# A hinted branch, doubles loaded behind the experts' weights, and conversions kept in their written place, in a fused attention and FFN kernel

## The chip, the cores and the metric

One core of one Trainium2 chip runs the whole program in one launch. The metric is the device time of an execution in microseconds (us). The engines are named as in the profile: PE (TensorE, matmul; PEld its weight loads, PEq or PEldq its sequencer's own rows), DVE (VectorE), ACT (ScalarE), POOL (GpSimd) and SP (the engine that issues the DMAs here).

## The reference

Four batches of 576 tokens go through an attention with random features (8 heads of 64), a layer with 8 experts of which each token takes one, and a gated FFN:

```
q_p, k_p = phi(q), phi(k)                       # exp of a projection on 128 features
attn = (q_p @ (k_p.T @ v)) / (q_p @ sum(k_p) + 1e-6)
x = attn as 2304 x 512
idx = argmax(x_normed @ emb_normed.T / tau);  gate = softmax value at idx
for e in range(8): y[idx == e] = gate * (relu(x @ w1[e]) @ w2[e])     # 512 -> 1024 -> 512
out = (silu(y @ w_gate) * (y @ w_val)) @ w_out                        # 512 -> 1536 -> 512
```

## The kernel before, in words

**Stages.** Attention and routing fill the first 165 us or so. For each batch the routing finds on the chip the expert that takes most tokens (`dom_i`) and how many tokens go to other experts (`tot_i`, their total). Then the dominant expert of each batch runs over all 576 tokens of it, one after the other (`expert`, four times). Tokens of other experts are done by `extras`: an `If` on `totals[0] > 0` with loops over batches and experts in its body. For the data here the total is zero, so the body never runs. It stands in the program between expert 0 and expert 1. Then comes phase 3 (L1069), gate and value product of the FFN in a form with seven products, in NF = 12 slices f of the hidden width, and phase 4 (L1114), the output product with 648 matmuls of 128x512.

**Precision.** A product of floats is three matmuls on pairs of reduced-precision operands. `hi_lo` makes a pair: ACT casts (L92), DVE subtracts (L93). The weights of an expert come as floats, one raw DMA of 512 KB per unit (`Expert.fetch`, L375) and one pair of L92 and L93. An expert has four units for its first layer (`mm1`, L856, each 2 x 24 matmuls) and four groups of 48 matmuls for its second (`mm2`, L875), each followed by `gated` (DVE product L887 or L890, POOL addition L888). The weights of phases 3 and 4 arrive as 64-bit floats ("doubles"): `convert` (L746) loads two of them, 512 KB each, and `words` turns them to floats with one ACT operation (L759) and six of DVE (L760 to L778). `split_y` makes the operands of phase 3 from an expert's output `y` (names `xp`, `h_all` and `over_y` on L92, L93, and L916 for the differences).

**What sets the order.** Instructions are written by a program and then placed by a scheduler, which may move one ahead of others on its engine if its inputs allow. `keep_in_program_order` takes one from this freedom. Within an engine the placed order is fixed. Hooks (`todo`) call `extras`, `ahead`, `split...`, `weights_ahead` and `seven` between the units of an expert, keyed by batch and unit. An `If` is a compare and branch on each engine (L940); with `preferred_fallthrough_block=False` the block of the false case, which holds semaphore steps and a far jump to the join, follows directly behind the compare, and the body comes after it.

**Names.** `two` and `third` are pairs of PSUM banks that `mm1` and `mm2` use in turn; `a`, `b`, `c` are the banks of phase 3; `raw` a weight's DMA buffer, `raw64` that of two doubles, `cv_t` the conversion's scratch, `wp` a pair of expert weights, `wh`, `wl`, `over_y` pairs of weights of phase 3; `h` an input tile of phase 4 read back from DRAM (`hds`). `seven(f)` makes the sums and pairs of the weights of slice f.

Of the kernel before, what the change touches and what calls it, by code (L numbers as in the profile page):

```python
# [10 lines left out]
F32 = mybir.dt.float32  # L11
# [17 lines left out]
def attention_moe_ffn_kernel(  # L29
# [59 lines left out]

    def hi_lo(hi, lo, src, lo_eng=nc.vector):  # L90

        nc.scalar.copy(hi, src)  # L92
        lo_eng.tensor_tensor(out=lo, in0=src, in1=hi.bitcast(F32), op=ALU.subtract)  # L93
# [254 lines left out]
    why = "counts and indices worked out on the chip lie in this range"  # L348
    late = {}
    n_pair = [0]  # L350
# [7 lines left out]
    class Expert:  # L358
# [13 lines left out]
        def fetch(self, low=nc.vector):  # L372
            raw = wpool.tile([128, NC * FU], F32, tag="raw", name="raw")
            src = w12[bass.ds(self.e, 1), self.n]
            nc.sync.dma_start(out=raw, in_=src.rearrange("o p f -> p (o f)"))  # L375
            if self.extra:
                w = late["cpool"].tile([128, 2, NC * FU], F32R, tag="wp", name="wp")
            else:
                w = pair_tile()
            hi_lo(w[:, 0], w[:, 1], raw, low)  # L380
            self.ready.append(w)
            self.n += 1
# [359 lines left out]
    def convert(key, *doubles, at=None):  # L742

        raw = late["w"].tile([128, 2, DM, 2], I32, tag="raw64", name="raw64")
        for j, (f, m) in enumerate(doubles):
            nc.sync.dma_start(  # L746
                out=raw[:, j], in_=w64[f, m].bitcast(I32).rearrange("p (n w) -> p n w", w=2)
            )
        if at is None:
            at = late["w"].tile([128, 2, DM], F32, tag="w32", name="w32", bufs=2)  # L750
        w32[key] = at
        n = late["n"]
        for j in range(0, 2, n):
            words(at[:, j:j + n], raw[:, j:j + n], n)

    def words(w, raw, n):
        low, high = raw[:, :, :, 0].bitcast(U32), raw[:, :, :, 1]
        t = late["t"].tile([128, n, DM], I32, tag="raw", name="cv_t")
        nc.scalar.activation(out=t.bitcast(F32), in_=high.bitcast(F32), func=AF.Abs)  # L759
        nc.vector.tensor_scalar(  # L760
            out=t.bitcast(F32), in0=t.bitcast(F32), scalar1=F64_ZERO, scalar2=None, op0=ALU.max
        )
        nc.vector.tensor_scalar(
# [53 lines left out]
    with ExitStack() as p2:  # L817
# [51 lines left out]
        def mm2(x, hs):  # L869
            w = x.weights(128)  # L870
            ps = (banks if x.extra else pair)()[:, :, 0:HB]
            for f, h in enumerate(hs):
                for n, (a, b) in enumerate(HALVES):
                    for j in range(2):
                        nc.tensor.matmul(  # L875
                            ps[:, j], w[:, a, f, :], h[:, b, j * HB:(j + 1) * HB],
                            start=(f == 0 and n == 0), stop=(f == len(hs) - 1 and n == 2),
                        )
            return ps

        def gated(x, ps, d, add):
# [7 lines left out]
            else:  # L889
                nc.vector.tensor_tensor(out=yv, in0=ps, in1=gv, op=ALU.mult)  # L890

# [14 lines left out]
        def split_y(bt):  # L906
# [5 lines left out]
            def put(q, src):  # L912
                hi_lo(factor(bt, q, 0), factor(bt, q, 1), src)

# [19 lines left out]
        def extras():  # L934
            xs[1].fetch()
            routed.close()
            late["w"] = early.enter_context(
                tc.tile_pool(name="early", bufs=1, side="right", reuse_waits="tile")
            )
            with tc.If(totals[0] > 0, preferred_fallthrough_block=False):  # L940
                for bt in range(B):
# [19 lines left out]
        def ahead(bt):  # L961
            xs[bt - 1].fetch()
            xs[bt] = Expert(bt)
            xs[bt].fetch()

        def split(bt, runs):
            parts_at[bt] += runs
# [12 lines left out]
        def split2():  # L980
# [3 lines left out]
        todo = {  # L984
            (0, 0): routing_end, (0, NU - 1): no_y, (0, NU + NC - 1): extras,
            (1, NU - 1): split0,
# [3 lines left out]
        for bt in range(B):  # L990
            hooks = {u: go for (b, u), go in todo.items() if b == bt}
            if bt < LAST:
                hooks[NU + NC - 2] = lambda: ahead(bt + 1)
# [220 lines left out]
```

## Time and profile before

| what | value |
|---|---|
| time, median of 3 runs | 799.65 us (799.28 to 800.25) |
| the profiled execution | 802.45 us, of which 800.7 us are the span of the trace |
| mean granted clock of PE | 0.985 |
| PE busy | 767.9 us, 96% of the span |
| DVE, ACT, POOL busy | 64%, 46%, 18% of the span |
| DMA | 94.12 MB, 118 GB/s on average |

PE is the engine that is busy nearly always; the others have room on average. So the rows to read are those of the places where PE stood, and of what stood on the other engines there.

### The profile page before, as it was taken

Reading aid. Unit: us, or ns where it says so; the run is one execution under the profiler, and the core shown is the slowest. Engines: PE = TensorE matmul, PEld = TensorE weight load, DVE = VectorE, ACT = ScalarE, POOL = GpSimd, SP = SyncE. Lnnn points to the kernel's source line nnn. Section 1 sums busy time; section 2 is a strip of 40 time slices with the busy share of each in tenths; the row PEclk is TensorE's granted clock in tenths of the full one; section 3 lists DMA queues with packets and bytes.
Section 4 is the critical chain, followed back from the end, with each engine's and each line's share of the span. In section 5 each row is a group of like instructions: output and inputs, shape, how many; then the busy total and the mean of one; then the engine's idle time right before and its main releaser. Section 6 shows DMA issues by size and latency. Waiting matters only on the chain. (4 is left out here: it accounts for less than half of the span.)

```text
span 800.7 us, 16008 instructions
## 1 busy us (share of the span) xinstructions
PE 767.9 (96%) x6364; PEld 718.4 (90%) x6365; DVE 515.9 (64%) x937; ACT 368.2 (46%) x856; POOL 144.3 (18%) x197
## 2 busy tenths in 40 slices
PE   9999889999599999997999999999999999999998
PEld 8778778899499999997999999999999978888886
DVE  5788999573478655586877776877877693222220
ACT  5798578571244341343555444544454632232231
POOL 3865354200001102002021111221221110000000
PEclk9999999999799999998999999999999999999999
DMA  8644642232524322401143122423433253363323
GB/s 255 225 145 153 203 160 81 65 94 72 149 69 160 106 82 94 102 27 54 32 158 117 70 80 106 165 90 105 160 117 110 86 191 108 103 202 92 101 93 117
DMA packets 35643, 94.12 MB, mean 118 GB/s; under 512 B 4432, under 2 KB 8544, under 8 KB 35560
## 3 DMA queue, kind: packets, MB, share of 16 engines
q1 hardware_dynamic: 35400, 92.99, 35.9%
q8 instruction: 52, 0.85, 0.4%
q14 instruction: 31, 0.25, 0.1%
q10 hardware_dynamic: 160, 0.02, 0.0%
HBM read 74.05 MB, written 18.95 MB: 116 GB/s over the span
## 5 line engine op out<-in xcount | busy, mean ns | idle before, releaser
L1114 PE MATMUL o_ps<-xp 128*128 128x512 f32 x648 | 147.1, 389 | 0.0
L1114 PEld LDWEIGHTS o_ps<-xp 128*128 128x128 f32 x648 | 121.6, 188 | 25.2
L93 DVE TENSOR_TENSOR xp<-h,xp 128x1024 fp32r<-128x1024 f32 (+1 forms) x36 | 34.2, 957 | 99.1 <-ACT xp L92 98.6
L492 ACT ACTIVATE ph<-two,bias 128x128 f32<-128x128 f32 x288 | 78.2, 389 | 31.1 <-DVE bias L483 20.0
L856 PE MATMUL two<-xp,wp 128*128 128x288 f32 x576 | 81.7, 301 | 9.8 <-issue 5.8
L1041 POOL TENSOR_TENSOR cc<-c,cc 128x288 f32<-128x288 f32 x48 | 48.9, 1031 | 227.5 <-issue 201.8
L856 PEld LDWEIGHTS two<-xp,wp 128*128 128x128 f32 x576 | 79.5, 193 | 10.2 <-issue 6.0
L92 ACT CAST xp<-h 128x1024 fp32r<-128x1024 f32 (+1 forms) x36 | 30.0, 838 | 95.4 <-PE o_ps L1114 78.2
L1037 ACT ACTIVATE cc<-cc 128x288 f32<-128x288 f32 x96 | 42.1, 446 | 62.3 <-DVE cc L1034 54.3
L92 ACT CAST wp<-raw 128x1024 fp32r<-128x1024 f32 x32 | 33.6, 1049 | 54.9 <-PE two L875 29.8
L1069 PE MATMUL a<-xp,over_y 128*128 128x288 f32 x360 | 57.3, 295 | 0.0
L888 POOL TENSOR_TENSOR y_f<-y_f,t 128x576 f32<-128x576 f32 x13 | 19.1, 1473 | 200.8 <-DVE t L887 200.8
L1069 PE MATMUL a<-xp,wh 128*128 128x288 f32 x240 | 50.4, 300 | 4.5 <-DVE t L887 4.5
L93 DVE TENSOR_TENSOR wp<-raw,wp 128x1024 fp32r<-128x1024 f32 x30 | 47.0, 1567 | 10.2 <-ACT wp L92 9.8
L875 PE MATMUL third<-h_all,wp 128*128 128x288 f32 x384 | 52.8, 296 | 0.0
L875 PE MATMUL two<-h_all,wp 128*128 128x288 f32 x384 | 52.0, 295 | 0.0
L875 PEld LDWEIGHTS third<-h_all,wp 128*128 128x128 f32 x384 | 51.7, 189 | 0.0
L875 PEld LDWEIGHTS two<-h_all,wp 128*128 128x128 f32 x384 | 51.4, 189 | 0.0
L1069 PEld LDWEIGHTS a<-xp,over_y 128*128 128x128 f32 x360 | 50.8, 188 | 0.3 <-ACT s L1056 0.2
L475 DVE TENSOR_REDUCE mx<-two 128x8 f32<-128x1024 f32 x36 | 43.9, 1219 | 9.8 <-PE two L465 9.4
L1069 PEld LDWEIGHTS a<-xp,wh 128*128 128x128 f32 x240 | 39.4, 193 | 4.7 <-DVE t L887 4.7
L1034 DVE TENSOR_TENSOR cc<-c,s 128x288 f32<-128x288 f32 x48 | 21.8, 453 | 30.3 <-DMA hds<-cc 26.5
(222 smaller groups left out, 1558.0 us busy)
## 6 DMA issues: line engine op xcount, KB each, us to landing
raw<-in_w_dram SPq DMA_DIRECT2D x68, 512.0 KB, 3.8
hds<-cc SPq DMA_DIRECT2D x48, 288.0 KB, 3.1
h<-hds SPq DMA_DIRECT2D x24, 512.0 KB, 3.5
q<-in_qx_dram SPq DMA_DIRECT2D x18, 512.0 KB, 3.9
k<-in_kx_dram SPq DMA_DIRECT2D x14, 512.0 KB, 3.8
v<-in_vx_dram SPq DMA_DIRECT2D x18, 276.0 KB, 3.9
out_dram<-o SPq DMA_DIRECT2D x18, 256.0 KB, 3.3
h<-hds SPq DMA_DIRECT2D x12, 128.0 KB, 2.1
```

The lines of the kernel that those rows point to most:

```text
L92: nc.scalar.copy(hi, src)
L93: lo_eng.tensor_tensor(out=lo, in0=src, in1=hi.bitcast(F32), op=ALU.subtract)
L475: nc.vector.tensor_reduce(out=mx.rearrange("p (c a) -> p a c", a=2), in_=p.rearrange("p a (h m) -> p a h m", m=M), axis=AX.X, op=ALU.max,)
L492: nc.scalar.activation(out=ph[:, h, :], in_=p[:, h % 2, h // 2 * M:(h // 2 + 1) * M], func=AF.Exp, bias=bias[:, h:h + 1],)
L856: nc.tensor.matmul(ps[:, j], w[:, a, c, f * 128:(f + 1) * 128], xv[:, c, b, j * HB:(j + 1) * HB], start=(c == 0 and n == 0), stop=(c == NC ...
L875: nc.tensor.matmul(ps[:, j], w[:, a, f, :], h[:, b, j * HB:(j + 1) * HB], start=(f == 0 and n == 0), stop=(f == len(hs) - 1 and n == 2),)
L888: nc.gpsimd.tensor_tensor(out=yv, in0=yv, in1=t, op=ALU.add)
L1034: nc.vector.tensor_tensor(out=out, in0=ps, in1=other, op=ALU.add)
L1037: nc.scalar.activation(out=x, in_=x, func=AF.Silu)
L1041: nc.gpsimd.tensor_tensor(out=cc[:, 1], in0=c22, in1=cc[:, 1], op=ALU.mult)
L1069: nc.tensor.matmul(bank_of[k], wf[f][a][:, (wq * 2 + c) * 128:(wq * 2 + c + 1) * 128], factor(bt, xq, x)[:, c], start=(k not in begun), st ...
L1114: nc.tensor.matmul(p, h[:, x, i * 128:(i + 1) * 128], wos[f][:, a], start=(f == 0 and k == 0), stop=(f == NF - 1 and k == 2),)
```

## The change

The block of the false case of the `If` now follows its default place, behind the body and next to the join, and the branch has a label. A new hook, `near_extras`, runs one group of `mm2` ahead of `extras`; it does the weight fetches that came there and in `extras`, and puts a branch hint for the label on SP, PE and DVE, each directly behind an instruction that `late["mark"]` remembers for that engine. In `convert` the loads of doubles keep their written place while the experts run (`late["n"] == 1`). In `words` the ACT operation and the first DVE operation keep their written place. In `split_y` the first of the casts keeps its own.

```diff
--- before.py
+++ after.py
@@ -87,9 +87,11 @@
         n_banks[0] += 1
         return third() if n_banks[0] % 3 == 0 else banks()
 
-    def hi_lo(hi, lo, src, lo_eng=nc.vector):
-
-        nc.scalar.copy(hi, src)
+    def hi_lo(hi, lo, src, lo_eng=nc.vector, pinned=False):
+
+        go = nc.scalar.copy(hi, src)
+        if pinned:
+            tc.keep_in_program_order(go)
         lo_eng.tensor_tensor(out=lo, in0=src, in1=hi.bitcast(F32), op=ALU.subtract)
 
 
@@ -346,7 +348,7 @@
 
     ENG = mybir.EngineType
     why = "counts and indices worked out on the chip lie in this range"
-    late = {}
+    late = {"mark": {}}
     n_pair = [0]
 
     def pair_tile():
@@ -372,7 +374,9 @@
         def fetch(self, low=nc.vector):
             raw = wpool.tile([128, NC * FU], F32, tag="raw", name="raw")
             src = w12[bass.ds(self.e, 1), self.n]
-            nc.sync.dma_start(out=raw, in_=src.rearrange("o p f -> p (o f)"))
+            late["mark"][ENG.SP] = nc.sync.dma_start(
+                out=raw, in_=src.rearrange("o p f -> p (o f)")
+            )
             if self.extra:
                 w = late["cpool"].tile([128, 2, NC * FU], F32R, tag="wp", name="wp")
             else:
@@ -743,9 +747,11 @@
 
         raw = late["w"].tile([128, 2, DM, 2], I32, tag="raw64", name="raw64")
         for j, (f, m) in enumerate(doubles):
-            nc.sync.dma_start(
+            go = nc.sync.dma_start(
                 out=raw[:, j], in_=w64[f, m].bitcast(I32).rearrange("p (n w) -> p n w", w=2)
             )
+            if late["n"] == 1:
+                tc.keep_in_program_order(go)
         if at is None:
             at = late["w"].tile([128, 2, DM], F32, tag="w32", name="w32", bufs=2)
         w32[key] = at
@@ -756,10 +762,12 @@
     def words(w, raw, n):
         low, high = raw[:, :, :, 0].bitcast(U32), raw[:, :, :, 1]
         t = late["t"].tile([128, n, DM], I32, tag="raw", name="cv_t")
-        nc.scalar.activation(out=t.bitcast(F32), in_=high.bitcast(F32), func=AF.Abs)
-        nc.vector.tensor_scalar(
+        tc.keep_in_program_order(
+            nc.scalar.activation(out=t.bitcast(F32), in_=high.bitcast(F32), func=AF.Abs)
+        )
+        tc.keep_in_program_order(nc.vector.tensor_scalar(
             out=t.bitcast(F32), in0=t.bitcast(F32), scalar1=F64_ZERO, scalar2=None, op0=ALU.max
-        )
+        ))
         nc.vector.tensor_scalar(
             out=t, in0=t, scalar1=0x07FFFFFF, scalar2=3,
             op0=ALU.bitwise_and, op1=ALU.logical_shift_left,
@@ -872,7 +880,7 @@
             for f, h in enumerate(hs):
                 for n, (a, b) in enumerate(HALVES):
                     for j in range(2):
-                        nc.tensor.matmul(
+                        late["mark"][ENG.PE] = nc.tensor.matmul(
                             ps[:, j], w[:, a, f, :], h[:, b, j * HB:(j + 1) * HB],
                             start=(f == 0 and n == 0), stop=(f == len(hs) - 1 and n == 2),
                         )
@@ -887,7 +895,9 @@
                 nc.vector.tensor_tensor(out=t, in0=ps, in1=gv, op=ALU.mult)
                 nc.gpsimd.tensor_tensor(out=yv, in0=yv, in1=t, op=ALU.add)
             else:
-                nc.vector.tensor_tensor(out=yv, in0=ps, in1=gv, op=ALU.mult)
+                late["mark"][ENG.DVE] = nc.vector.tensor_tensor(
+                    out=yv, in0=ps, in1=gv, op=ALU.mult
+                )
 
         def expert(x, add, hooks=()):
 
@@ -910,7 +920,7 @@
             b21, b22 = y[:, 2:4, 0:HB], y[:, 2:4, HB:S]
 
             def put(q, src):
-                hi_lo(factor(bt, q, 0), factor(bt, q, 1), src)
+                hi_lo(factor(bt, q, 0), factor(bt, q, 1), src, pinned=q == 0)
 
             def sub(out, x, y):
                 nc.vector.tensor_tensor(out=out, in0=x, in1=y, op=ALU.subtract)
@@ -932,12 +942,11 @@
         totals, ends = [], []
 
         def extras():
-            xs[1].fetch()
             routed.close()
             late["w"] = early.enter_context(
                 tc.tile_pool(name="early", bufs=1, side="right", reuse_waits="tile")
             )
-            with tc.If(totals[0] > 0, preferred_fallthrough_block=False):
+            with tc.If(totals[0] > 0, label="extras"):
                 for bt in range(B):
                     with tc.For_i(0, E) as e:
                         n = nc.values_load(
@@ -963,6 +972,13 @@
             xs[bt] = Expert(bt)
             xs[bt].fetch()
 
+        def near_extras():
+            ahead(1)
+            xs[1].fetch()
+            for eng, ins in late["mark"].items():
+                with tc.issue_after(ins.ins):
+                    tc.mark_branch_hint_location("extras", "LikelyTaken", engines=[eng])
+
         def split(bt, runs):
             parts_at[bt] += runs
             ends.append(split_y(bt))
@@ -982,14 +998,15 @@
             split(2, own + [over_h(0), over_h(1)])
 
         todo = {
-            (0, 0): routing_end, (0, NU - 1): no_y, (0, NU + NC - 1): extras,
+            (0, 0): routing_end, (0, NU - 1): no_y,
+            (0, NU + NC - 2): near_extras, (0, NU + NC - 1): extras,
             (1, NU - 1): split0,
             (2, 0): lambda: weights_ahead(0), (2, NU - 1): split1,
             (3, 0): lambda: weights_ahead(1), (3, NU - 1): split2, (3, NU + 1): lambda: seven(0),
         }
         for bt in range(B):
             hooks = {u: go for (b, u), go in todo.items() if b == bt}
-            if bt < LAST:
+            if 0 < bt < LAST:
                 hooks[NU + NC - 2] = lambda: ahead(bt + 1)
             expert(xs[bt], bt > 0, hooks)
         next(ends[2], None)
```

PE around the branch, before: the end of expert 0, the load of the total, the two branches of the `If` (L940), and, past the body, expert 1.

```order
L875 MATMUL two<-h_all,wp 128x288 x96
L875 MATMUL third<-h_all,wp 128x288 x48
L953 TENSOR_LOAD tot_i
L940 COMPARE_AND_BRANCH
L940 UNCONDITIONAL_BRANCH
...
L942 REGISTER_ALU
L942 COMPARE_AND_BRANCH
L942 UNCONDITIONAL_BRANCH
L856 MATMUL two<-xp,wp 128x288 x48
```

After (the `If` is L949, `mm2` L883, `mm1` L864):

```order
L883 MATMUL two<-h_all,wp 128x288 x96
L1227 BRANCH_PREFETCH_HINT
L883 MATMUL third<-h_all,wp 128x288 x48
L962 TENSOR_LOAD tot_i
L949 COMPARE_AND_BRANCH
...
L951 COMPARE_AND_BRANCH
L951 UNCONDITIONAL_BRANCH
L949 UNCONDITIONAL_BRANCH
L864 MATMUL two<-xp,wp 128x288 x48
```

The hint stands between the last two groups of `mm2`; the unconditional branch has gone from behind the compare, and one stands behind the body.

DVE at the end of expert 3, before: conversion steps (L760 to L778), the split of y (L93, L916) and the last two products (L887).

```order
L774 SCALAR_TENSOR_TENSOR cv_t<-raw_7015 128x1024
L778 TENSOR_TENSOR w_7018<-w_7018,cv_t 128x1024
L93 TENSOR_TENSOR h_all<-y_f,h_all 128x576 x2
L916 TENSOR_TENSOR y_f<-y_f 128x2x288
L760 TENSOR_SCALAR cv_t<-cv_t 128x1024
L93 TENSOR_TENSOR h_all<-y_f,h_all 128x576
L763 TENSOR_SCALAR cv_t<-cv_t 128x1024
L887 TENSOR_TENSOR t<-two,gate 128x576
L887 TENSOR_TENSOR t<-third,gate 128x576
```

After (split L95 and L926, products L895):

```order
L95 TENSOR_TENSOR wp<-raw,wp 128x1024
L95 TENSOR_TENSOR h_all<-y_f,h_all 128x576 x2
L926 TENSOR_TENSOR y_f<-y_f 128x2x288
L95 TENSOR_TENSOR h_all<-y_f,h_all 128x576
L895 TENSOR_TENSOR t<-two,gate 128x576
L895 TENSOR_TENSOR t<-third,gate 128x576
L926 TENSOR_TENSOR y_f<-y_f 128x2x288
```

The conversion steps are gone from ahead of and between the splits; the last two products stand next to each other as before, with one split ahead of them.

DVE at the start of phase 4, before: the last two evictions of phase 3 (L1040), one conversion, the splits of two w pairs and of the input tiles h, which go on alone from there.

```order
L1040 TENSOR_TENSOR cc<-a,cc 128x288
L760 TENSOR_SCALAR cv_t<-cv_t 128x1024
...
L778 TENSOR_TENSOR w_10201<-w_10201,cv_t 128x1024
L93 TENSOR_TENSOR xp<-w_10201,xp 128x512 x2
L93 TENSOR_TENSOR xp<-h_10094,xp 128x1024
L93 TENSOR_TENSOR xp<-h_10138,xp 128x1024
L93 TENSOR_TENSOR xp<-h_10166,xp 128x1024
```

After (L1057; conversions L768 to L786):

```order
L1057 TENSOR_TENSOR cc<-a,cc 128x288 x2
L768 TENSOR_SCALAR cv_t<-cv_t 128x1024
L771 TENSOR_SCALAR cv_t<-cv_t 128x1024
...
L786 TENSOR_TENSOR w_9984<-w_9984,cv_t 128x1024
L95 TENSOR_TENSOR xp<-h_10097,xp 128x1024
L95 TENSOR_TENSOR xp<-w_9984,xp 128x512 x2
L768 TENSOR_SCALAR cv_t<-cv_t 128x1024
...
L95 TENSOR_TENSOR xp<-h_10141,xp 128x1024
L775 SCALAR_TENSOR_TENSOR w_10132<-raw_10129,cv_t 128x1024
...
L95 TENSOR_TENSOR xp<-h_10169,xp 128x1024
L95 TENSOR_TENSOR xp<-w_10132,xp 128x512 x2
L768 TENSOR_SCALAR cv_t<-cv_t 128x1024
...
L95 TENSOR_TENSOR xp<-h_10213,xp 128x1024
L775 SCALAR_TENSOR_TENSOR w_10204<-raw_10201,cv_t 128x1024
...
L95 TENSOR_TENSOR xp<-h_10241,xp 128x1024
```

Three conversions now stand among the splits of h, where one stood ahead of them. On SP the loads of the first doubles moved likewise, from behind the gates of expert 1 to behind the first weight load of expert 2.

## Rows read from the trace of the kernel before

**Rows 1.** Page, busy us of each engine (share of the span), number of instructions.

```profile
PE 767.9 (96%) x6364; PEld 718.4 (90%) x6365; DVE 515.9 (64%) x937; ACT 368.2 (46%) x856; POOL 144.3 (18%) x197
```

**Rows 2.** What PE waited for: sum of us, times, longest.

```profile
PE two L856 <- issue: 5.8, 1, 5.8
PE a L1069 <- DVE t L887: 4.5, 1, 4.5
PE two L856 <- ACT xp L92: 3.9, 1, 3.9
...
PE a L1069 <- DVE c L1034: 1.5, 2, 1.0
PE a L1069 <- ACT u L1058: 1.4, 1, 1.4
```

**Rows 3.** Timeline of PE, 190 to 232: start, us, count, [idle before, releaser].

```profile
189.72 10.29 PE L875 MATMUL two<-h_all,wp 128*128 128x288 f32 x76
199.86 6.56 PE L875 MATMUL third<-h_all,wp 128*128 128x288 f32 x48
210.33 1.57 PE L856 MATMUL two<-xp,wp 128*128 128x288 f32 x7 [3.92 <-ACT xp L92]
217.76 7.08 PE L856 MATMUL two<-xp,wp 128*128 128x288 f32 x41 [5.85 <-issue]
224.68 3.36 PE L856 MATMUL third<-xp,wp 128*128 128x288 f32 x24
```

**Rows 4.** By windows: busy us and counts of engines, PEclk, DMA share, GB/s.

```profile
212.00:224.00 12.00, 6.24 (x36) 6.24 (x36) 4.29 (x6) 1.03 (x2) 0.00 (x0) 0.62 0.45 143
...
371.00:385.00 14.00, 9.55 (x55) 9.32 (x54) 8.44 (x13) 5.35 (x11) 2.80 (x2) 0.76 0.00 0
385.00:540.00 155.00, 155.00 (x1172) 154.79 (x1172) 119.15 (x219) 75.98 (x177) 27.43 (x28) 1.00 0.30 105
```

**Rows 5.** Instructions of L940, the `If`: ns min/median/max, first to last start.

```profile
L940 DVEq COMPARE_BRANCH  x2: 51/53/55, 201.8 to 202.6; - x2
...
L940 PEldq COMPARE_BRANCH  x2: 95/1752/3410, 204.5 to 206.8; - x2
L940 PEldq EVENT_SEMAPHORE  x2: 51/51/51, 206.5 to 206.6; - x2
```

**Rows 6.** DMA issues by SP, 196 to 232.

```profile
202.55 1.07 SPq L375 DMA_DIRECT2D raw<-in_w_dram  x2
...
209.24 0.98 SPq L746 DMA_DIRECT2D raw<-in_w_dram  x2
```

**Rows 7.** Timeline of PE, 360 to 386.

```profile
370.63 1.20 PE L875 MATMUL third<-h_all,wp 128*128 128x288 f32 x8
376.29 0.85 PE L1069 MATMUL a<-xp,wh 128*128 128x288 f32 x2 [4.45 <-DVE t L887]
...
381.49 0.45 PE L1069 MATMUL c<-over_y,wh 128*128 128x288 f32 x2
```

**Rows 8.** Timeline of DVE, 366 to 384.

```profile
371.24 0.70 DVE L760 TENSOR_SCALAR cv_t<-cv_t 128x1024 f32<-128x1024 f32 x1 [2.78 <-ACT cv_t L759]
...
373.12 0.75 DVE L887 TENSOR_TENSOR t<-two,gate 128x576 f32<-128x576 f32 x1
375.47 0.76 DVE L887 TENSOR_TENSOR t<-third,gate 128x576 f32<-128x576 f32 x1 [1.60 <-POOL y_f L888]
```

**Rows 9.** Timeline of POOL, 370 to 384.

```profile
374.05 1.40 POOL L888 TENSOR_TENSOR y_f<-y_f,t 128x576 f32<-128x576 f32 x1 [11.28 <-DVE t L887]
```

**Rows 10.** Timeline of PE, 553 to 558.

```profile
556.15 1.07 PE L1069 MATMUL a<-h_all,over_y 128*128 128x288 f32 x6 [1.39 <-ACT u L1058]
```

**Rows 11.** Timeline of DVE, 640 to 700: first and last step of one conversion.

```profile
652.81 0.70 DVE L760 TENSOR_SCALAR cv_t<-cv_t 128x1024 f32<-128x1024 f32 x1 [0.21 <-ACT cv_t L759]
...
658.00 1.23 DVE L778 TENSOR_TENSOR w<-w,cv_t 128x1024 f32<-128x1024 f32 x1
```

**Rows 12.** Timeline of DVE, 640 to 700: a split of an h tile.

```profile
667.33 1.22 DVE L93 TENSOR_TENSOR xp<-h,xp 128x1024 fp32r<-128x1024 f32 x1 [3.59 <-ACT xp L92]
```

## The prediction

> **What bounds the kernel now.** I read the page's table of busy time first: TensorE (PE) is busy 767.9 of 800.7 us [rows 1], so 32.8 us are the most that filling its gaps can return (a slower clock behind a gap comes on top). Second came the list of what PE waited for: the three largest entries, 5.8 us on "issue", 4.5 us on DVE's product `t`, 3.9 us on "ACT xp" [rows 2], are single events, and they are the ones this change touches. The other entries lie in the attention stage, which the change leaves alone, or are short ones at the end of a phase. Third, the PE timeline around the two places where these three stand, and fourth the other engines there.
>
> *Place one, the branch behind expert 0.* The last group of expert 0 starts at 199.86; at 0.133 us a matmul (10.14 us for the 76 before it) its 48 end at 206.26, and the first 48 of expert 1 could be through at 212.66. The group behind those starts at 224.68 [rows 3]. The loss is 12.0 us: two idle stretches, 3.92 and 5.85, and 2.25 us of slow running (granted clock 0.62 in 212 to 224 [rows 4], where 1.00 is the upper of the two levels, 2.4 GHz, and the lower, 1.2 GHz, is 0.50). The rows of the `If` tell what the first stretch is. The compare at 204.5 must be the one of 0.095 us, since the semaphore steps start 2 us later; so the other branch, from 206.8, took 3.41 us, to 210.2, and PE's first matmul is at 210.33. DVE's two, at 201.8 to 202.6, show 0.05 us [rows 5]. The timeline blames "ACT xp", but the program's first matmul there needs nothing of ACT that late; I read the row of the branch: PE's instructions come from far away and must be fetched. "Issue" in front of the second stretch says the same: seven matmuls ran, and then nothing was left to issue. Meanwhile SP had issued two weight loads at 202.55 and, at 209.24, 1 MB of doubles [rows 6].
>
> *Place two, expert 3 to phase 3.* mm2 ends at 370.63 + 8 x 0.133 = 371.70. L1069 starts at 376.29 and is through 21 matmuls at 381.49, where 21 x 0.133 from 371.70 would give 374.50 [rows 7]: 7.0 us lost, 4.45 of it idle, the rest again the clock (0.76 over 371 to 385 [rows 4]). The chain is DVE: a step of a doubles conversion at 371.24 that waited 2.78 for ACT, more work behind it, then `t<-two` at 373.12 though `two` was long done, POOL's addition 1.40, and only then `t<-third` at 375.47, whose bank L1069 needs [rows 8, 9].
>
> **The change, part by part.** Durations are of the profiled execution, 802.45 us; the sum is made there, and the median of the runs, 799.65, is 2.80 below it, which I take off at the end.
>
> *Branch and hint.* The block of semaphore steps now lies behind the body, beside the join, so PE takes one far branch, at the compare (204.5), and not a second at 206.8; the join follows it directly. The hint stands 48 matmuls ahead of the end, some 6.4 us before PE's compare, nearly twice the 3.41 of a far branch [rows 5]. If the target is there at 204.6, the sequencer waits only for the end of the matmuls (206.4), and 0.3 us of steps remain. The next fetch can start at 204.6 and not behind 210; priced as the only one the rows show, 3.41, it ends at 208.0. Seven pairs take 0.93 from 206.5, so PE is idle about 0.5; I add 0.5 for restart and clock. New loss 1.5 in round numbers, gain 10.5. Bounds: 0.3 lost (gain 11.7) where the second fetch is in time too; 9.6 lost where the hint does nothing (branch to 207.9, 1.5 behind the matmuls) and the second stretch stays with its clock, 5.85 + 2.25 (gain 2.4). I take 1.5, since the stretch of 5.85 had the doubles' megabyte beside it, which has gone. The hint, `ahead(1)` and the fetch that moved cost nothing: PE runs its 48 matmuls there, and SP's raw loads keep their order. ACT and POOL get no hint, so theirs may now be a far branch of 3.41 too. DVE, which comes to its compare at 201.8, would by that be ready near 205.2 even without its hint, ahead of PE's step at 206.5 for which all wait, and ACT and POOL come to theirs before DVE: nothing is lost there.
>
> The Trainium skill ("Runtime: NRT & Kernel Launch", section "Instruction fetch mechanics") says that prefetch is purely sequential and that a taken branch whose target is outside the two-page window has to fetch the page before execution goes on; it knows of no hint. The 3.41 us row agrees with the stall. By the rule the hint buys nothing, which is the first rival below.
>
> *Doubles behind the experts' weights.* 1 MB leaves the queue at 209 and is loaded in expert 2 instead. On SP it was ahead of three weight loads, so these come earlier; PE waited for no weights in the experts [rows 2]. In experts 2 and 3 the doubles' loads wait for buffers that are free by then. Cost 0, with the gain already in the fetch; were an expert's weights late behind the megabyte, it would be a wait like the one added below.
>
> *Casts of the split of y in place.* ACT does two and not four xp casts right behind the join, and the relus come earlier. PE waited for neither outside the branch [rows 2]: 0.
>
> *Conversions in place.* At the end of expert 3, DVE has no conversion step before `t<-two`. The last `two` matmul is now 13 matmuls from the end, not 8: 371.70 - 1.73 = 369.97. DVE 0.75 from 370.1, hand-over 0.18 (373.12 + 0.75 to 374.05), POOL 1.40, DVE 0.76 [rows 8, 9]: `t<-third` is through near 373.2, PE starts at 373.3, idle 1.6. The idle stretch of 1.39 in front of 556.15 was followed by six matmuls in 1.07 us, near their full rate [rows 10], so I take no slow clock: loss 1.6 for 7.0, gain 5.4. Bounds: 3.0 where the clock falls again (7.0 - 4.45 = 2.5 lost), 5.4 as the chain cannot be shorter.
>
> What moves later must fit. A conversion at a stretch took DVE from 652.81 to 659.23, 6.4 us [rows 11]. In phase 3, 385 to 540, DVE is busy 119.15 of 155.00, with 1172 matmuls, 0.132 us each [rows 4]. An f is 168 matmuls, 22.2 us, of which DVE is free for 5.1 (its idle 35.85 of 155). The conversion is in its busy time already and only starts about half an f later, right behind the pair of batches 2 and 3; the half f of 11.1 us that it then has until the next sums of weights are due holds its 6.4 beside evictions. In phase 4 three conversions now stand among DVE's splits of h, each 6.4 us against a gap of 3.59 ahead of a split of 1.22 [rows 12]. From the order of the program a split stands about two h tiles, 10 us, ahead of its matmuls, and DVE falls behind by some 2.8 a tile (6.4 - 3.6), three times, so 8.4: just covered. I add one wait of the size of the 1.39 [rows 10] for all of this: cost 1.4. Bounds: -2.9, where the short waits of phase 3 (1.4 on ACT `u`, 1.5 in two on DVE `c` [rows 2]) go, to 6.4, one whole conversion in the open.
>
> **Sum.** 10.5 + 5.4 - 1.4 = 14.5; 802.45 - 14.5 = 787.95; less 2.80: **785.2 us**.
>
> **Rivals.** *The hint buys nothing*: PE fetches the target only once the branch is taken. Compare at 204.5 + 3.41 = 207.9, 1.5 behind the matmuls; the second fetch 3.41 less 0.93 is 2.5 more; 1.0 of clock, half of what was lost: 5.0 lost, gain 7.0, in all 11.0: 788.7. For it: the branch row; against: loop hints are already in this program, and there are 6.4 us of lead. This is what the rule quoted above from the Trainium skill would make of the change. *The change does not do what it says at the branch*: the second stretch is a fetch behind weight traffic (the weight loads of 202.55 stay), and stays: gain 2.4 + 5.4 - 1.4 = 6.4, 793.3. For it: the word "issue" and 5.85, longer than any fetch needs alone; against: the megabyte has gone. *Slower: pinned conversions hold DVE in phases 3 and 4.* Place: the evictions of `a`, `b`, `c` queue behind the conversion's steps, and PE waits for a bank. At 1.39 for each of some 13 conversions it is 18.1 against 15.9: +2.2, 801.9; it decides from 15.9 / 13 = 1.22 a conversion. For it: DVE is 77% busy there, and PE already waited for DVE's `c` there [rows 2]; against: only the first two steps are pinned, the others still interleave. At half that price, 792.7.
>
> **Numbers.** Forecast 0.48, no hint 0.25, second stretch stays 0.12, conversions at half price or nearly so 0.06, at full price or more 0.09. Under 0.2% (1.6 us) nothing can be told from no change. Faster 0.88, same 0.03, slower 0.09. The likeliest one's own range is 781 to 789. The range for 8 in 10 goes from 780.5 (all the best ends together, 11.7, 5.4 and 2.9, give 779.7) to 795.5, past the second rival.
>
> **What would show it.** PE's timeline behind the branch: idle under 1 and under 1.5 us, and a clock of 0.9 or more in the 12 us behind it; a PE compare row of 0.1 us (hint works) or about 3.4 (it doesn't). L1069's first wait: near 1.6 us, on DVE `t`, with POOL's addition near 371. Phase 3's list of waits: none that repeats with each f. Phase 4: PE idle 0 in the first 50 us. I am wrong if the branch still loses over 6 us, or if L1069 or L1114 shows waits by the dozen.

## The result, and the profile after

The changed kernel takes 780.68 us (median of four runs, 779.93 to 782.13), the kernel before 799.95 beside it: ratio 0.9755, 95% interval 0.9726 to 0.9783. That is 19.3 us faster where 14.5 were forecast. The time stands at the lower end of the range (780.5); by the ratio, 799.65 x 0.9755 = 780.1, it is just under it. The profiled execution took 782.13 us, its span 780.4 against 800.7, and the account below is made of the two spans.

PE's row of the page: 780.4 - 762.6 = 17.8 us of the span are idle, where 32.8 were [rows 1], and the busy time itself fell by 5.3.

```profile
PE 762.6 (98%) x6364; PEld 714.4 (92%) x6365; DVE 515.4 (66%) x937; ACT 370.5 (47%) x856; POOL 138.9 (18%) x197
```

What PE waited for (sum, times, longest), the rows that answer to [rows 2]; the lines that are left out belong to the attention and routing stages (the first 165 us). The "issue" entry and "ACT xp" are gone, the first wait of phase 3 is a third of what it was, and "ACT u" is gone inside phase 3:

```profile
PE a L1086 <- DVE t L895: 1.5, 1, 1.5
...
PE two L864 <- PEq L949: 0.4, 1, 0.4
...
PE a L1086 <- DVE c L1051: 0.3, 1, 0.3
```

PE's timeline at the branch, the answer to [rows 3] (start, us, count, idle before and its end):

```profile
199.37 6.56 PE L883 MATMUL third<-h_all,wp 128*128 128x288 f32 x48
206.38 6.89 PE L864 MATMUL two<-xp,wp 128*128 128x288 f32 x48 [0.45 <-PEq L949]
213.10 3.36 PE L864 MATMUL third<-xp,wp 128*128 128x288 f32 x24
```

The last group of expert 0 starts at 199.37, so the first 48 of expert 1 could be through at 199.37 + 12.80 = 212.17; the next group starts at 213.10. The loss is 0.93 us where it was 12.02: one idle stretch of 0.45, and of the second one 0.10 by the starts of the single matmuls, too short for a row of its own. The granted clock of this stretch is 1.00; the same stretch before, 199.86 to 224.68, had 0.79, with the 0.62 of [rows 4] in it:

```profile
199.37:213.10 13.73, 13.19 (x98) 12.88 (x97) 6.06 (x7) 3.80 (x5) 1.42 (x1) 1.00 0.48 110
```

The rows of the `If`, as in [rows 5] (ns min/median/max, first to last start): PE's compare, now its only branch, takes 0.48 us, where the far jump took 3.41, and its semaphore steps come at 206.0, right behind the end of the matmuls.

```profile
L949 DVEq EVENT_SEMAPHORE  x2: 21/21/21, 204.2 to 204.3; - x2
L949 PEldq EVENT_SEMAPHORE  x2: 51/51/51, 206.0 to 206.1; - x2
...
L949 DVEq COMPARE_BRANCH  x1: 84/84/84, 201.3 to 201.3; - x1
L949 PEldq COMPARE_BRANCH  x1: 481/481/481, 204.0 to 204.0; - x1
```

PE's hint, in the same form, was executed 7.0 us ahead of that compare:

```profile
L1227 PEldq BRANCH_PREFETCH_HINT  x1: 50/50/50, 197.0 to 197.0; - x1
```

The end of expert 3, PE as in [rows 7], then DVE as in [rows 8] and POOL as in [rows 9]:

```profile
358.56 1.88 PE L883 MATMUL third<-h_all,wp 128*128 128x288 f32 x13
361.95 0.54 PE L1086 MATMUL a<-xp,wh 128*128 128x288 f32 x2 [1.50 <-DVE t L895]
...
364.83 0.42 PE L1086 MATMUL c<-over_y,wh 128*128 128x288 f32 x2
```

```profile
357.07 0.76 DVE L95 TENSOR_TENSOR h_all<-y_f,h_all 128x576 fp32r<-128x576 f32 x1 [0.79 <-ACT h_all L92]
358.76 0.76 DVE L895 TENSOR_TENSOR t<-two,gate 128x576 f32<-128x576 f32 x1 [0.94 <-PE two L883]
361.13 0.76 DVE L895 TENSOR_TENSOR t<-third,gate 128x576 f32<-128x576 f32 x1 [1.61 <-POOL y_f L896]
```

```profile
359.69 1.41 POOL L896 TENSOR_TENSOR y_f<-y_f,t 128x576 f32<-128x576 f32 x1 [9.60 <-DVE t L895]
```

The matmuls end at 358.56 + 13 x 0.133 = 360.29, PE waits 1.50, and 21 matmuls of phase 3 are through at 364.83, where 363.09 would be without loss: 1.74 us lost, before 7.0. No conversion step stands among DVE's rows, and the matmuls run at full rate at once.

Counted from group to group, with the same instructions between, the spans differ as follows:

| stretch | before | after | difference |
|---|---|---|---|
| start to expert 0's last group | 199.86 | 199.37 | -0.49 |
| to the third 24 of expert 1 | 24.82 | 13.73 | -11.09 |
| to the end of expert 3's matmuls | 147.02 | 147.19 | +0.17 |
| to 21 matmuls of phase 3 | 9.79 | 4.54 | -5.25 |
| to the first matmul of phase 4 | 268.40 | 264.75 | -3.65 |
| to the end | 150.81 | 150.82 | +0.01 |

### The profile page after: what moved, and what is told of

It is laid out like the page before. It is cut to its first block, busy times and chain, and to the rows that moved or that the text cites. A ratio compares the mean times of both kernels' runs of the same rounds, so it can differ in the third digit from the quotient of the medians.

```text
span 780.4 us, 16006 instructions
## 1 busy us (share of the span) xinstructions
PE 762.6 (98%) x6364; PEld 714.4 (92%) x6365; DVE 515.4 (66%) x937; ACT 370.5 (47%) x856; POOL 138.9 (18%) x197
## 4 chain that ended last, share of the span: by engine, by line
PE 70%; issue 2%; DVE 0%; DMA 0%; POOL 0%; ACT 0%; POOLq 0%; ACTq 0%; DVEq 0%
PE o_ps L1131 19%; PE a L1086 18%; PE b L1086 9%; PE two L864 7%; PE two L883 5%; PE third L883 5%; PE c L1086 5%; PE third L864 2%; DMA hds<-cc 0%; DVE t L895 0%; POOL y_f L896 0%; DVE xp L95 0%; POOL cc L1058 0%; ACT o L1138 0%; ACT p L1076 0%
## 5 line engine op out<-in xcount | busy, mean ns | idle before, releaser
L95 DVE TENSOR_TENSOR xp<-h,xp 128x1024 fp32r<-128x1024 f32 (+1 forms) x36 | 34.4, 957 | 80.8 <-ACT xp L92 80.3
L1058 POOL TENSOR_TENSOR cc<-c,cc 128x288 f32<-128x288 f32 x48 | 41.0, 865 | 226.3 <-issue 205.0
L864 PE MATMUL two<-xp,wp 128*128 128x288 f32 x576 | 79.9, 297 | 0.5 <-PEq L949 0.4
L864 PEld LDWEIGHTS two<-xp,wp 128*128 128x128 f32 x576 | 77.6, 189 | 0.9 <-issue 0.9
L1086 PE MATMUL a<-xp,over_y 128*128 128x288 f32 x360 | 59.0, 295 | 0.0
L896 POOL TENSOR_TENSOR y_f<-y_f,t 128x576 f32<-128x576 f32 x13 | 21.6, 1662 | 184.2 <-DVE t L895 153.2
L95 DVE TENSOR_TENSOR wp<-raw,wp 128x1024 fp32r<-128x1024 f32 x30 | 47.2, 1573 | 9.6 <-ACT wp L92 9.0
L883 PE MATMUL third<-h_all,wp 128*128 128x288 f32 x384 | 52.8, 296 | 0.0
L883 PE MATMUL two<-h_all,wp 128*128 128x288 f32 x384 | 52.2, 296 | 0.0
L883 PEld LDWEIGHTS third<-h_all,wp 128*128 128x128 f32 x384 | 51.7, 189 | 0.0
L883 PEld LDWEIGHTS two<-h_all,wp 128*128 128x128 f32 x384 | 51.5, 189 | 0.0
L1051 DVE TENSOR_TENSOR c<-a,p 128x288 f32<-128x288 f32 x48 | 21.6, 455 | 24.2 <-PE a L1086 24.1
```

Of the source, the lines that this page charges most:

```text
L864: nc.tensor.matmul(ps[:, j], w[:, a, c, f * 128:(f + 1) * 128], xv[:, c, b, j * HB:(j + 1) * HB], start=(c == 0 and n == 0), stop=(c == NC ...
L883: late["mark"][ENG.PE] = nc.tensor.matmul(ps[:, j], w[:, a, f, :], h[:, b, j * HB:(j + 1) * HB], start=(f == 0 and n == 0), stop=(f == len ...
L896: nc.gpsimd.tensor_tensor(out=yv, in0=yv, in1=t, op=ALU.add)
L1051: nc.vector.tensor_tensor(out=out, in0=ps, in1=other, op=ALU.add)
L1058: nc.gpsimd.tensor_tensor(out=cc[:, 1], in0=c22, in1=cc[:, 1], op=ALU.mult)
L1086: nc.tensor.matmul(bank_of[k], wf[f][a][:, (wq * 2 + c) * 128:(wq * 2 + c + 1) * 128], factor(bt, xq, x)[:, c], start=(k not in begun), st ...
```

## The experiments

Theories: the hint removes the branch's stall (A) or the new place of the false block does (B); the doubles' megabyte lengthens the second stretch (C); the pinned conversions give what is gained at the start of phase 3 and in it (D). "Loss" at the branch is always the start of the third 24 of expert 1 less (start of expert 0's last group + 12.80). All ratios are to the kernel before on the same chip.

**Without hints.**

```diff
-            for eng, ins in late["mark"].items():
-                with tc.issue_after(ins.ins):
-                    tc.mark_branch_hint_location("extras", "LikelyTaken", engines=[eng])
```

> The changed kernel without its three branch hints (SP, PE, DVE). Theory 'hint': PE's compare row grows from 0.48 to about 3.4 us, the first idle stretch behind the branch from 0.45 to about 2 us, and a second one of 1 to 3 us comes back; loss at the branch 4 to 6 us instead of 0.9, about 784 to 786 us. Rival 'layout': the one far branch less is what counts; loss under 1.5 us, about 781 us.

787.52 us, ratio 0.9818 (0.9798 to 0.9839). PE's timeline and its compare:

```profile
200.14 6.56 PE L883 MATMUL third<-h_all,wp 128*128 128x288 f32 x48
209.19 1.30 PE L864 MATMUL two<-xp,wp 128*128 128x288 f32 x8 [2.50 <-PEq L949]
214.72 7.19 PE L864 MATMUL two<-xp,wp 128*128 128x288 f32 x40 [4.22 <-issue]
221.75 3.36 PE L864 MATMUL third<-xp,wp 128*128 128x288 f32 x24
```

```profile
L949 PEldq COMPARE_BRANCH  x1: 3912/3912/3912, 204.7 to 204.7; - x1
```

Both stretches are back, 2.50 and 4.22, behind a compare of 3.91 us; loss 221.75 - 212.94 = 8.81. Beside the stretches that is 2.1 us, of which the changed kernel has 0.4 too, at full clock, as restart around a stretch; the other 1.7 or so are slow running. The profiled execution, 791.62 us, is the longest of five (786.05 to 791.62), so 8.81 stands at the upper end. A holds, and more of the time hung on the hint than expected. B has a part: 12.0 has become 8.8.

**Hints with the old place of the false block.**

```diff
-            with tc.If(totals[0] > 0, label="extras"):
+            with tc.If(totals[0] > 0, preferred_fallthrough_block=False, label="extras"):
```

> The changed kernel with its hints but the false case's block directly behind the compare again, with the far jump behind it. Theory 'hint carries, layout not': loss at the branch under 1.5 us, about 781 us. Rival 'layout needed': the hint names the compare's target and the jump behind the block stays far; PE stands 3.4 us at the jump and loses 5 to 9 us at the branch, about 785 to 789 us.

791.22 us, ratio 0.9857 (0.9818 to 0.9897).

```profile
L949 PEldq COMPARE_BRANCH  x2: 104/1972/3839, 204.2 to 206.6; - x2
```

```profile
199.62 6.56 PE L883 MATMUL third<-h_all,wp 128*128 128x288 f32 x48
210.56 1.84 PE L864 MATMUL two<-xp,wp 128*128 128x288 f32 x7 [4.38 <-ACT xp L92]
216.12 7.89 PE L864 MATMUL two<-xp,wp 128*128 128x288 f32 x41 [3.71 <-issue]
223.84 3.36 PE L864 MATMUL third<-xp,wp 128*128 128x288 f32 x24
```

The loss is 223.84 - 212.42 = 11.42, nearly the old 12.0 and more than the 5 to 9 expected: the far jump behind the block took 3.84 us, hint or not. So neither edit of the branch does the work of both: the place alone leaves 8.8 of 12.0, the hint alone 11.4, both 0.9.

**Hints one group later**: PE's stands behind the last matmul ahead of the `If`, and so 0.9 us ahead of its compare, where 7.0 stood.

```diff
         def extras():
...
+            for eng, ins in late["mark"].items():
+                with tc.issue_after(ins.ins):
+                    tc.mark_branch_hint_location("extras", "LikelyTaken", engines=[eng])
             with tc.If(totals[0] > 0, label="extras"):
...
         def near_extras():
...
-            for eng, ins in late["mark"].items():
-                with tc.issue_after(ins.ins):
-                    tc.mark_branch_hint_location("extras", "LikelyTaken", engines=[eng])
```

> The changed kernel with the hints set one group of matmuls later, behind the last matmul (PE) ahead of the If, so that PE's hint has some 0.5 us of lead over its compare in place of about 6. Theory 'lead': the target is still on its way; compare row 3 to 3.5 us, first stretch about 2 us, second 1 to 4 us, loss 4 to 8 us, 784 to 789 us. Rival 'any hint': the fetch of what follows the target starts with the hint, too, and both stretches stay short; loss under 2 us.

788.04 us, ratio 0.984 (0.9801 to 0.9878).

```profile
L1227 PEldq BRANCH_PREFETCH_HINT  x1: 50/50/50, 202.3 to 202.3; - x1
```

```profile
L952 PEldq COMPARE_BRANCH  x1: 3510/3510/3510, 203.1 to 203.1; - x1
```

```profile
207.11 1.16 PE L864 MATMUL two<-xp,wp 128*128 128x288 f32 x7 [2.29 <-PEq L952]
211.27 8.09 PE L864 MATMUL two<-xp,wp 128*128 128x288 f32 x41 [3.00 <-issue]
219.20 3.36 PE L864 MATMUL third<-xp,wp 128*128 128x288 f32 x24
```

The compare takes 3.51 us and both stretches are there; loss 219.20 - (198.26 + 12.80) = 8.14, as without hints within a microsecond. What such a hint saves is no more than its lead.

**PE's hint alone**, without those of SP and DVE.

```diff
-            for eng, ins in late["mark"].items():
+            for eng, ins in [(ENG.PE, late["mark"][ENG.PE])]:
```

> The changed kernel with PE's hint alone, none on SP and DVE. Theory 'only PE's branch is on the path': loss at the branch stays near 0.9 to 1.3 us, 781 us, though DVE's and SP's compare may grow to about 3.5 us; DVE's next work waits for PE's step at about 206 anyway. Rival 'DVE and SP need theirs': SP's gates and weight loads come 3 us later or DVE's splits do, and PE waits 1 to 3 us behind the branch.

781.74 us, ratio 0.9755 (0.973 to 0.978). Compares of DVE and SP, and the rows that follow them:

```profile
L949 SPq EVENT_SEMAPHORE  x9: 17/17/17, 192.7 to 193.3; - x9
...
L949 DVEq EVENT_SEMAPHORE  x2: 21/21/21, 202.8 to 202.9; - x2
...
L949 SPq COMPARE_BRANCH  x1: 50/50/50, 188.5 to 188.5; - x1
...
L949 DVEq COMPARE_BRANCH  x1: 72/72/72, 200.0 to 200.0; - x1
```

PE's stretches are 0.45 and 0.91, loss 1.74: the other engines' hints are worth nothing that can be told. The compares take 0.05 and 0.07 us without a hint, but a short row is not a short branch: DVE's next row comes 2.9 us behind its compare and SP's 4.1, as in the changed kernel with their hints (DVE 201.3 to 204.2, though its hint had come at 193.2). PE does not wait for it. "Theirs may now be a far branch of 3.41 too" was said of ACT and POOL; their next rows come 0.5 us behind their compares of 0.045 us, so for them it was wrong.

**Doubles free**, once with the hints and once without.

```diff
-            if late["n"] == 1:
-                tc.keep_in_program_order(go)
```

> The changed kernel with the loads of doubles free to move (they go back behind the gates of expert 1, ahead of its weights). Theory 'traffic': the second stretch of the kernel before (5.85 us on issue) was a fetch queued behind this megabyte; it comes back with 2 to 5 us, about 783 to 786 us. Rival 'hint alone': the target and what follows it are there in time anyway; loss at the branch stays near 0.9 us, about 781 us.

> The changed kernel without hints and with the doubles' loads free, so back at the branch: of the branch edits only the new place of the false case's block is left. Theory 'traffic lengthens the second fetch': the second idle stretch grows from 4.22 us (without hints, doubles behind) toward the 5.85 of the kernel before, loss at the branch 10 to 11 us, 1 to 2 us slower than without hints alone. Rival 'traffic does not matter': second stretch stays 4.2 us, loss about 8.8 us.

With hints 781.24 us, ratio 0.9748 (0.973 to 0.9766), loss 212.41 - 211.24 = 1.17: nothing came back. Without hints 788.81 us, ratio 0.9856 (0.9816 to 0.9897):

```profile
197.91 6.56 PE L881 MATMUL third<-h_all,wp 128*128 128x288 f32 x48
206.78 1.30 PE L862 MATMUL two<-xp,wp 128*128 128x288 f32 x8 [2.31 <-PEq L947]
210.64 8.20 PE L862 MATMUL two<-xp,wp 128*128 128x288 f32 x40 [2.57 <-issue]
218.68 3.36 PE L862 MATMUL third<-xp,wp 128*128 128x288 f32 x24
```

The second stretch is 2.57, shorter than the 4.22 with the doubles out of the way, loss 7.97. That does not settle C. In the kernel before, SP issued the doubles from 209.24 on, ahead of the end of PE's far jump (206.8 + 3.41 = 210.2 [rows 5, 6]); here it does so from 206.48 on, behind the end of the compare (206.32), so the megabyte does not stand ahead of what PE fetches next. With the false block in its old place the second stretch is 5.85 and 5.88 with the megabyte (the kernel before, and the one with pinned conversions alone) and 3.71 without it (hints with the old place, which has other edits too): C stays open.

What the stretch is can be read from the DMA records of these traces. The packets of 16 KB in the instruction queue (q8 of the page, 52 in a run) come every 17 us or so while the experts run and fit PE's stops, so I take them for PE's instructions. Around the branch, start to end:

| kernel | taken branch of PE | packet of its target | next packet | PE goes on |
|---|---|---|---|---|
| before | 206.76 to 210.17 | 207.73 to 208.84 | 215.56 to 216.56 | 217.76 |
| hints, old place of the block | 206.56 to 210.40 | 208.00 to 209.05 | 213.66 to 214.63 | 216.12 |
| without hints | 204.75 to 208.66 | 205.76 to 207.22 | 211.03 to 213.32 | 214.72 |
| without hints, doubles free | 202.53 to 206.32 | 203.54 to 204.92 | 208.17 to 209.16 | 210.64 |
| changed | 203.99 to 204.47 | 200.24 to 201.31 | 205.25 to 206.29 | 207.64 |

The second stretch ends 1.2 to 1.5 us behind the next packet, so I take it for the wait for the instructions that follow. In the six kernels without a hint in time, that packet starts 1.4 to 5.5 us behind the end of the branch, with the DMA engines 84% busy or more in between; in the eight with one, it starts 0.7 to 0.8 us behind the end of the compare (DMA share 0.04 in the changed kernel), while matmuls of expert 0 still run. The packet of the target itself starts 2.9 to 3.6 us behind PE's hint there and is through before the compare; with the old place of the block no packet follows the hint (197.2) before the far jump, which fits its doing nothing there. That the other transfers hold the next packet back is likely and not tested.

**Conversions free.**

```diff
-        tc.keep_in_program_order(
-            nc.scalar.activation(out=t.bitcast(F32), in_=high.bitcast(F32), func=AF.Abs)
-        )
-        tc.keep_in_program_order(nc.vector.tensor_scalar(
+        nc.scalar.activation(out=t.bitcast(F32), in_=high.bitcast(F32), func=AF.Abs)
+        nc.vector.tensor_scalar(
             out=t.bitcast(F32), in0=t.bitcast(F32), scalar1=F64_ZERO, scalar2=None, op0=ALU.max
-        ))
+        )
```

> The changed kernel with the conversions' ACT step and first DVE step free to move again. Theory 'pinned conversions': conversion steps stand again ahead of the last products of expert 3, the first wait of phase 3 is 4 to 5 us with a slow clock behind it, and the short waits inside phase 3 (1.39, 1.03, 0.44) come back: 5 to 8 us more, about 786 to 789 us. Rival 'other edits': the shift of the loads or of the split's casts is what cleared that place; about 781 us.

786.66 us, ratio 0.9818 (0.9787 to 0.9849). What PE waited for behind the attention stage:

```profile
PE a L1084 <- DVE t L893: 3.3, 1, 3.3
...
PE a L1084 <- DVE c L1049: 1.5, 2, 1.0
...
PE b L1084 <- ACT p L1074: 0.5, 1, 0.5
...
PE two L862 <- PEq L947: 0.4, 1, 0.4
...
PE a L1084 <- ACT u L1073: 0.2, 1, 0.2
```

The first wait is 3.28, not 4 to 5, and nothing ran slowly behind it (clock 1.00 in 358 to 372): 21 matmuls end at 365.28 for 361.79, loss 3.49. Inside phase 3 2.2 us of waits are back. D holds in kind. In size, counted from group to group, 1.8 us of the way into phase 3 and 2.9 inside it (to 632.98, where phase 4 starts) are back, 4.7 of the 8.9 that the whole change gained there; why not all of it isn't shown.

**Conversions pinned in the kernel before, nothing else.** The same edit, the other way.

> The kernel before with one edit alone: the conversions' ACT step and first DVE step keep their written place. Theory 'pinned conversions': the first wait of phase 3 falls from 4.45 to about 1.5 us with no slow clock behind it, the waits inside phase 3 (1.39, 1.03, 0.44) nearly go, and the branch is as before with its 12 us: 8 us less in all, about 0.990 of the time before. Rival 'only with the rest': the conversions land elsewhere without the shifted loads, and under half of the 8 us comes.

793.33 us, ratio 0.9903 (0.9864 to 0.9942). Span 793.0, 7.7 less than before:

```profile
PE two L858 <- issue: 5.9, 1, 5.9
PE two L858 <- ACT xp L92: 4.3, 1, 4.3
...
PE a L1071 <- DVE t L889: 1.5, 1, 1.5
...
PE a L1071 <- DVE c L1036: 0.5, 1, 0.5
```

The branch is as before (5.9 and 4.3); the first wait of phase 3 is 1.5, "ACT u" is gone, `c` is 0.5. Counted from group to group, the way into phase 3 is 5.3 us shorter than in the kernel before and phase 3 itself 3.5 (377.26 to 642.18): 8.7 of the 8.9 of the whole change. D holds, and this one edit gives nearly all of it. With the 11.1 of the branch that is 19.8 of the 20.3 us between the profiles. The two do not hang on each other: here the branch is not mended, and with the conversions free it loses 211.82 - 198.29 - 12.80 = 0.73.

**Only ACT's step pinned.**

```diff
-        tc.keep_in_program_order(nc.vector.tensor_scalar(
+        nc.vector.tensor_scalar(
             out=t.bitcast(F32), in0=t.bitcast(F32), scalar1=F64_ZERO, scalar2=None, op0=ALU.max
-        ))
+        )
```

> The changed kernel in which only ACT's conversion step keeps its written place and DVE's first step is free. Theory 'ACT's step is the one that matters, since DVE's steps need its result': waits as in the changed kernel (first wait of phase 3 about 1.5 us, no repeat inside), 781 us. Rival 'DVE's own place matters': DVE's first step moves ahead of evictions and stands there waiting for ACT, PE waits 1 to 3 us more in phase 3.

780.43 us, ratio 0.9736 (0.9713 to 0.9759), first wait 1.51, none on `c`. Keeping DVE's first step in place adds nothing: ACT's step carries the others.

**First cast of the split free.**

```diff
-                hi_lo(factor(bt, q, 0), factor(bt, q, 1), src, pinned=q == 0)
+                hi_lo(factor(bt, q, 0), factor(bt, q, 1), src, pinned=False)
```

> The changed kernel with the first cast of the split of y free to move again. Theory: PE waited for none of these outside the branch, so the time is that of the changed kernel, ratio to before 0.975 within its interval, no wait of PE over 0.5 us that the changed kernel has not. Rival 'ACT late behind the join': four casts (2.5 us) stand ahead of the first weight cast and relu behind the join, and PE waits 1 to 2 us there now that the branch no longer covers them.

781.14 us, ratio 0.9757 (0.9719 to 0.9795); loss at the branch 211.69 - 210.42 = 1.27, first wait of phase 3 1.51. This edit does nothing that can be told.

**A scratch of its own for the last product.**

```diff
-                t = tp.tile([128, S], F32, tag="t", name="t")
+                if x.bt == LAST and d == NC - 1 and not x.extra:
+                    t = wpool.tile([128, NC * FU], F32, tag="raw", name="t")[:, 0:S]
+                else:
+                    t = tp.tile([128, S], F32, tag="t", name="t")
```

> The changed kernel with a scratch of its own for the very last product of expert 3 (a weight buffer that is free by then), so that DVE's last product needs not wait for POOL's addition. Theory 'the chain DVE, POOL, DVE makes the last 1.5 us': the first wait of phase 3 falls from 1.50 to about 0.8 us (end of the matmuls, one DVE product of 0.76), 0.7 us less, 0.1%, hardly to be told in the times but plain in the profile. Rival 'something else releases the bank': the wait stays 1.5 us.

780.84 us, ratio 0.9744 (0.9722 to 0.9765). DVE's two last products and PE's first wait:

```profile
357.89 0.76 DVE L898 TENSOR_TENSOR t<-two,gate 128x576 f32<-128x576 f32 x1 [0.94 <-PE two L883]
359.61 0.76 DVE L898 TENSOR_TENSOR t<-third,gate 128x576 f32<-128x576 f32 x1 [0.96 <-PE third L883]
```

```profile
360.42 0.54 PE L1089 MATMUL a<-xp,wh 128*128 128x288 f32 x2 [0.85 <-DVE t L898]
```

The second product now waits for PE and not for POOL; the wait is 0.85, as expected. In the times 0.65 us can't be told.

**A scratch of its own, and only ACT's step pinned:** the two diffs named so together.

> The changed kernel with both small steps of the runs before: a scratch of its own for the last product of expert 3, and only ACT's conversion step kept in place. If the two add, the first wait of phase 3 is 0.85 us and the 0.3 to 0.6 us on DVE's c at the end of phase 3 are gone: span about 778 us, some 1 us (0.1%) under the changed kernel, ratio to before 0.973 to 0.975. If they do not add, the ratio is that of the changed kernel, 0.9755, and its trace has the 1.5 us or the 0.3 us again.

780.30 us, ratio 0.973 (0.9705 to 0.9754); span 778.0, first wait 0.85, no wait on `c`. The two add in the trace, by the 0.65 and the 0.3 us of those waits; in the times the interval overlaps that of the changed kernel, so that it beats it isn't shown.

## Why the prediction was right or wrong, point by point

*The branch.* "New loss 1.5 in round numbers, gain 10.5": measured 0.93 and 11.1. The first stretch (0.3 forecast, 0.45) and the lead (6.4 us forecast, 7.0) were right, and the late hint shows that the lead decides. The second stretch was to be 0.5 and is 0.10; in the eight kernels with the hint in time it is 0 to 0.91, so the size was partly luck. The working behind it holds by the packets: "The next fetch can start at 204.6 and not behind 210"; its packet starts at 205.25, and PE goes on at 207.64 where 208.0 was worked out. The other reason, "the stretch of 5.85 had the doubles' megabyte beside it, which has gone", is not shown: in no run with the hint in time is the megabyte issued ahead of that packet.

*The rival "the hint buys nothing"* was priced at 5.0 lost; without hints 8.81 are. Its first stretch (1.5 for 2.50), its second (2.5 for 4.22) and the clock (1.0 for some 1.7) were too small. What was held against it, "loop hints are already in this program", had no row to rest on: the trace before has none of a hint, as the loops stand in the body that never runs. The rule of the Trainium skill ("Runtime: NRT & Kernel Launch", section "Instruction fetch mechanics"), that a taken branch with its target outside the window waits for a fetch, agrees with the compares of 3.4 to 3.9 us on PE wherever no hint came in time; where one did, 0.48 stands, which the rule does not foresee.

The rival "the second stretch is a fetch behind weight traffic" is near to what the packets show of the kernel before, with a start 5.4 us late; what it missed is that the hint lets this fetch start early.

*End of expert 3.* Gain 5.4 forecast, 5.25 measured; idle 1.6 forecast, 1.50 measured, with the chain DVE, POOL, DVE and POOL's addition in it (1.41). The scratch of its own confirms the chain: without POOL in it 0.85. No slow clock, as forecast.

*The step that failed* is "I add one wait of the size of the 1.39 [rows 10] for all of this: cost 1.4". The sign was wrong: phase 3 became 3.65 us shorter, past even the bound of -2.9 where its short waits go. Of these, 2.60 are idle time gone (1.39 + 1.03 + 0.44 before, 0.26 now). The rest of 1.05 is not idle time and not the clock, which was back at the upper level at 381.53, where this stretch begins. It lies in the starts of single matmuls: each such wait cost 0.27 us more in the starts at and behind it, and six starts elsewhere in phase 3 before were 0.7 us late together, which is about as much as is missing. I had read the short wait as a sample of what a pinned conversion may cost; its row on ACT in the kernel before shows that it was the cost of a free one (timeline of ACT):

```profile
551.33 0.38 ACT L1058 COPY u<-a 128x288 f32<-128x288 f32 x1
554.68 1.12 ACT L759 ACTIVATE cv_t<-raw 128x1024 f32<-128x1024 f32 x1 [2.97 <-DMA raw<-in_w_dram]
555.70 0.39 ACT L1058 COPY u<-a 128x288 f32<-128x288 f32 x1
```

The conversion's step stands in ACT's line ahead of the second copy `u` and waited 2.97 us for its doubles' DMA, and that `u` released PE at 556.15 [rows 10]. Kept in their written place, the steps mostly come when their data are there. What they waited for their DMA, before and after (sum, times, longest):

```profile
ACT cv_t L759 <- DMA raw<-in_w_dram: 20.2, 12, 4.8
```

```profile
ACT cv_t L766 <- DMA raw<-in_w_dram: 8.1, 4, 2.7
```

With the term at -2.6 for +1.4 the sum would have been 18.5, and 781.2.

*Slower rival.* "Pinned conversions hold DVE in phases 3 and 4": nothing of it. Phase 4 takes 150.81 before and 150.82 now, so the three conversions among the splits are covered, as worked out.

*Doubles and the split's casts* were put at 0, and are 0 in their runs.

## What to carry to other kernels

A far branch around a long body that never runs cost 3.4 to 3.9 us here on the engine that bounds the kernel, and a second wait for instructions behind it; a hint several microseconds ahead and a layout with a single far branch removed nearly all of it, and only together. Where "issue" ends an idle stretch, look at the packets of the instruction queue. A scheduler that lifts the first step of a side job ahead of critical work, on data that is still under way, turns a job that has room into a wait: the step that waits for the DMA is the one to pin. Where a short wait stands in the list, follow it to the instruction ahead in its engine's line before pricing what a change adds.

## What the runs showed that I had not expected

The hint on PE shortened the second stretch, too, seven or eight matmuls behind the join: 0 to 0.91 us are left in all eight kernels with it in time and the new layout, while the six others show 2.6 to 5.9 us there. On DVE and SP the row of the compare took 0.04 to 0.08 us with or without a hint, and in the new layout the next row came some 2.9 and 4.1 us behind it, hint or not; why a hint 8 us ahead did nothing for DVE stays open. The granted clock: behind the single waits of 1.50 and 3.28 us in front of phase 3 the matmuls ran at full rate (1.00, the level of 2.4 GHz). Behind 4.45 us, or behind the two stretches at the branch, part of the next matmuls ran at the lower level, 1.2 GHz (mean 0.76 and 0.62 in [rows 4]), also in the two kernels where each of the two was shorter than that 3.28 (2.29 and 3.00: mean 0.72 from 207.11 to 219.20; 2.31 and 2.57).
